# Fewer and differently issued loads at the start of a cached-attention decode kernel, and part of one multiply on GpSimd

## The chip, the cores and the metric

The kernel runs on one core of one Trainium2 chip. The metric is the device time of one execution in microseconds (us). The kernel before takes 1298.83 us (median of 3 runs, 1298.82 to 1298.9).

## The reference

One decode step for two rows of x (512 wide): attention of 32 heads over a cache of 8192 keys and values of 128 floats each, and an MLP whose SiLU gates the attention's output.

```python
def _A_ref(x, k_cache, v_cache, wq, wo):
    B, Sq, D = x.shape
    H, Dh = 32, 128
    q = (lambda x, *d: x.transpose(*d))((x @ wq).reshape(B, Sq, H, Dh), 0, 2, 1, 3)
    scores = jnp.einsum("bhqd,bhkd->bhqk", q, k_cache) * (Dh ** -0.5)
    p = _softmax(scores, axis=-1)
    o = jnp.einsum("bhqk,bhkd->bhqd", p, v_cache)
    return (lambda x, *d: x.transpose(*d))(o, 0, 2, 1, 3).reshape(B, Sq, H * Dh) @ wo

def _B_ref(x, w1, b1, w2, b2):
    y = _layernorm(x, axis=-1)
    h = _gelu(jnp.einsum("bsd,df->bsf", y, w1) + b1)
    return jnp.einsum("bsf,fd->bsd", h, w2) + b2

x = A_x
xn = _layernorm(x, axis=-1)
s = _A_ref(xn, A_k_cache, A_v_cache, A_wq, A_wo)
g = _silu(_B_ref(xn, B_w1, B_b1, B_w2, B_b2))
return x + s * g
```

Everything is float32. B is 2, D is 512, F is 1376.

## The kernel before

**Tiling.** The 64 head rows (2 batch rows of 32 heads) are worked in pairs: 32 pairs, n = 0 to 31. The keys of a pair are one tile `kb` of 128 partitions x 128 keys x 128 floats (64 KB in each partition), the values one tile `vb` of the same size. There are two `kb` buffers, which alternate (pair 0 uses the second, `kb1`), and one `vb` buffer. The first `kb` buffer holds the query weights wq until the query is made, and `vb` holds the MLP's weights w1 and w2, the biases and x, all with their scratch, until the MLP is done.

**One pair.** VectorE multiplies the keys by the query row in two halves of 64 keys (`scores_mul(n, 0)` and `(n, 1)`, L555), adds up each half over the 128 floats (`scores_sum`, L562) and takes the maximum (`max_rows`, L566). TensorE transposes the maximum (L569), VectorE makes it one number for each head (L572), ScalarE takes the exponentials (L583), and TensorE multiplies them with the values in 32 steps (`weighted`, L606).

**Order.** A planner (class `Plan`) writes each engine's operations in the order of the calls and puts in the waits that the data need. Pairs 1 to 30 run in a loop on each engine; the first and the last pair stand outside it. VectorE's order around the first pair is mul(0,0), mul(0,1), sum(0,0), sum(0,1), max(0), mul(1,0), L572 of pair 0, mul(1,1), and so on. So `weighted(0)` begins only after mul(1,0).

**Loads.** All loads are issued by SyncE (`load`, L329) into one queue, in the order w1, x, w2, b1, b2, wq, the first half and the second half of pair 0's keys (K0), then K1, V0, K2, V1, K3 and so on. K1 waits for the last TensorE operation that reads wq (L513), which stands in TensorE's order behind the whole MLP (L433 to L486). V0 waits for the last VectorE operation on the MLP's scratch and stands behind K1. K(n+2) waits for max(n), since its buffer is that of K(n); V(n) waits for `weighted(n-1)`. The last pair's keys and values come in two halves each, and the weights wo come last, in seven pieces.

**MLP and query.** x goes through two layer norms on VectorE and ScalarE (L380 to L385), TensorE transposes the results (L392), then come w1 with b1 (L433, L435), w2 with b2 (L475, L479), and the query (L513). ScalarE copies the query and spreads it to all partitions (L518, L528); mul(0,0) needs the first of these copies (`Q`, block 0) and K0's first half.

Of the kernel before, what the change touches and what calls it, by code (L numbers as in the profile page):

```python
# [5 lines left out]
ALU = mybir.AluOpType  # L6
# [155 lines left out]
                put(o, order(o.waits))  # L162


def decode_kernel(nc, x, kc, vc, wq, wo, w1, b1, w2, b2, out):
    P = 128
    B, H, S, DH = kc.shape
    D = x.shape[2]
    F = w1.shape[1]
    ND = D // P  # L170
    U = 2
    HP = P // U
    KP = S // HP
# [29 lines left out]
    def pe(fn, r=(), w=(), it=None, loop=False):  # L203
        op("pe", fn, r, w, it=it, loop=loop)
# [70 lines left out]
    def take(name, p, n, base=0, at=None):  # L275

        if at is None:
            at = used[0]
            used[0] += n
            assert used[0] <= KP * DH  # L280
        boot.append(name)
        return vb[base:base + p, at:at + n]

    w1_sb = take("w1", P, ND * F).rearrange("p (c f) -> p c f", f=F)
    w2_sb = take("w2", P, WB * P)

    at = used[0]
    take("rows", P, F + D)
    x_sb, xn, y = (take(k, B, D, 0, at + D * i) for i, k in enumerate(("x", "xn", "y")))
    b1_sb = take("b1", 1, F, R, at)  # L290
    b2_sb = take("b2", 1, D, R, at + F)
    h_row = take("h_row", B, WR * P, 2 * R, at).rearrange("b (r p) -> b r p", p=P)
    h_nat = take("h_nat", B, WB * R + WM * (QT - 1), 3 * R, at)
    hs = take("hs", P, WM * QT * QT * B).rearrange("p (a c j b) -> p a c j b", c=QT, j=QT, b=B)
# [29 lines left out]
    kf = kc.rearrange("b h s d -> (b h s d)").rearrange("(n p j d) -> n p j d", p=P, j=KP, d=DH)  # L324
    vf = vc.rearrange("b h s d -> (b h s d)").rearrange("(n p j d) -> n p j d", p=P, j=KP, d=DH)
    M = KP // 2

    def load(dst, src, sem, w, over=()):
        op("sp", lambda: nc.sync.dma_start(dst, src), (), w, over=over, dma=sem)  # L329

    def load_k(n):
        i = (n + 1) % 2
        if n in (0, N - 1):
            for s in range(2):
                load(kbuf[i][:, s * M:(s + 1) * M], kf[n][:, s * M:(s + 1) * M], f"k{i}{s}", [("kb", i, s)])
            return
        load(kbuf[i], kf[n], f"kb{i}", [("kb", i, s) for s in range(2)])
# [4 lines left out]
    CUT = D - P  # L342


    load(w1_sb, w1.rearrange("(p c) f -> p c f", p=P), "w1", ["w1"])
    load(x_sb, x.rearrange("b s d -> (b s) d"), "x", ["x"])
    load(w2_sb, w2.rearrange("f n -> (f n)").rearrange("(p e) -> p e", p=P), "w2", ["w2"])
    for t, src, k in ((b1_sb, b1, "b1"), (b2_sb, b2, "b2")):
        load(t.rearrange("o (k e) -> o k e", k=16), src.rearrange("(o k e) -> o k e", o=1, k=16), k, [k])
    load(wq_sb, wq.rearrange("(p c) n -> p c n", p=P), "wq", [("kb", 0, s) for s in range(2)])  # L350
    load_k(0)

# [73 lines left out]
    def mlp():  # L426

        chunks = range(0, F, 512)
        for f in chunks:
            w = min(512, F - f)  # L430
            ph, k = bank()
            for c in range(ND):
                pe(lambda f=f, w=w, ph=ph, c=c: matmul(ph[:B, :w], yT[:, c, :], w1_sb[:, c, f:f + w],  # L433
                                                       start=(c == 0), stop=False), ["yT", "w1"], [k])
            pe(lambda f=f, w=w, ph=ph: matmul(ph[:B, :w], ones[R:R + 1, :B], b1_sb[:, f:f + w],  # L435
                                              start=False, stop=True), ["ones", "b1"], [k])
            act(lambda f=f, w=w, ph=ph: nc.scalar.copy(h_nat[:, 1 + f:1 + f + w], ph[:B, :w]),  # L437
                [k, "h_nat"], [("h_nat", f)])

        for m in range(QT):  # L440
            dve(lambda m=m: nc.vector.tensor_copy(  # L441
                h_row[:, :, m::QT],
                h_nat[:, WM * m:WM * m + WB * R].rearrange("b (k e) -> b e k", e=WB)[:, :WR, :]),
                ["h_nat"] + [("h_nat", f) for f in chunks], [("h_row", m)])
        ph, k = bank()
        for r in range(WR):
            pe(lambda r=r: transpose(ph[:, r * B:(r + 1) * B], h_row[:, r, :], ident[2 * R:2 * R + B, 2 * R:2 * R + B]),
               ["ident"] + [("h_row", m) for m in range(QT)], [k])

        act(lambda: nc.scalar.copy(h, ph[:, :WR * B].rearrange("p (r b) -> p r b", b=B)), [k], ["h"])  # L450
        dve(lambda: nc.vector.tensor_mul(u, h, h), ["h"], ["u"])
        dve(lambda: nc.vector.tensor_scalar(u, u, GELU_A, 1.0, op0=ALU.mult, op1=ALU.add), ["u"], ["u"])
        dve(lambda: nc.vector.tensor_mul(u, u, h), ["u", "h"], ["u"])
        act(lambda: nc.scalar.activation(u, u, AF.Tanh, scale=GELU_C), ["u"], ["u"])  # L454
        dve(lambda: nc.vector.scalar_tensor_tensor(u, u, 1.0, h, op0=ALU.add, op1=ALU.mult), ["u", "h"], ["u"])
        dve(lambda: nc.vector.tensor_scalar_mul(u, u, 0.5), ["u"], ["u"])
        px, kx = bank()
        pe(lambda: matmul(px, pick, x_sb, start=True, stop=True), ["pick", "x"], [kx])
        act(lambda: nc.scalar.copy(xa, px), [kx], ["xa"])

        parts = []
        for c in range(QT):
            for lo, hi, r, m in ((0, c + 1, 1, QT - 1 - c), (c + 1, QT, 0, 0)):
                if lo == hi:
                    continue
                parts.append(("hs", c, lo))

                def part(c=c, lo=lo, hi=hi, r=r, m=m):
                    shape = [P, WM, hi - lo, B]
                    return nc.vector.tensor_tensor(  # L470
                        out=hs[:, :, c, lo:hi, :], in0=u[:, r:r + WM, :].unsqueeze(2).to_broadcast(shape),
                        in1=cls[:, m:m + hi - lo].unsqueeze(1).unsqueeze(3).to_broadcast(shape), op=ALU.mult)
                dve(part, ["u"] + [("cls", m) for m in range(QT)], [parts[-1]])
        pw, kw = bank()
        pe(lambda: matmul(pw[:R, :], b2w[R:R + 1, :], b2_sb, start=True, stop=False), ["b2w", "b2"], [kw])  # L475
        for a in range(WM):
            j = a % QT
            w = min(512, WB * P - a * 512)
            pe(lambda a=a, j=j, w=w: matmul(pw[R * j:R * (j + 1), :w], hs[:, a].rearrange("p c j b -> p (c j b)"),  # L479
                                            w2_sb[:, a * 512:a * 512 + w], start=(0 < a < QT), stop=(a + QT >= WM)),  # L480
               parts + ["w2"], [kw])
        act(lambda: nc.scalar.copy(g_sb, pw), [kw], ["g"])

        p, kp = bank()
        for c in range(QT):
            pe(lambda c=c: matmul(p[:, :P], fold[:, c, :], g_sb[:, c * P:(c + 1) * P], start=(c == 0), stop=(c == QT - 1)),  # L486
               ["fold", "g"], [kp])

        act(lambda: nc.scalar.copy(z, p[:, :P]), [kp], ["z"])
        act(lambda: nc.scalar.activation(th, z, AF.Tanh, scale=0.5), ["z"], ["th"])  # L490
        dve(lambda: nc.vector.scalar_tensor_tensor(th, th, 1.0, z, op0=ALU.add, op1=ALU.mult), ["th", "z"], ["th"])
        for j in range(QT):
            dve(lambda j=j: nc.vector.tensor_scalar_mul(
                gate[R * j:R * (j + 1), :, 1], th[R * j:R * (j + 1), j * CW:(j + 1) * CW], 0.5), ["th"], [("gate", j)])
        dve(lambda: nc.vector.tensor_tensor(
            out=xa.rearrange("p (q n) -> p q n", n=CW), in0=xa.rearrange("p (q n) -> p q n", n=CW),
            in1=slot.unsqueeze(2).to_broadcast([P, CH, CW]), op=ALU.mult), ["xa", "slot"], ["xa"])
        dve(lambda: nc.vector.tensor_reduce(out=x4, in_=xa.rearrange("p (q n) -> p n q", n=CW), axis=AX.X, op=ALU.add),
            ["xa"], ["x4"])

    mlp()


# [46 lines left out]

    def scores_mul(n, s):
        i = (n + 1) % 2
        k = kbuf[i][:, s * M:(s + 1) * M, :]
        qs = [("Q", 0)] if n == 0 else [("Q", b) for b in range(N // NB)]
        vector(n, n, lambda n: nc.vector.tensor_tensor(  # L555
            out=k, in0=k, in1=cols(Q, n * DH, DH).unsqueeze(1).to_broadcast([P, M, DH]), op=ALU.mult),
            [("kb", i, s)] + qs, [("kb", i, s)])

    def scores_sum(n, s):
        i = (n + 1) % 2  # L560
        k = kbuf[i][:, s * M:(s + 1) * M, :]
        vector(n, n, lambda n: nc.vector.tensor_reduce(out=SC[:, s * M:(s + 1) * M], in_=k, axis=AX.X, op=ALU.add),  # L562
               [("kb", i, s)], [("sc", s)])

    def max_rows(n):
        vector(n, n, lambda n: nc.vector.tensor_reduce(out=MX, in_=SC, axis=AX.X, op=ALU.max),  # L566
# [156 lines left out]
    plan.emit(HEADS)  # L723


_INS = ["A_x", "A_k_cache", "A_v_cache", "A_wq", "A_wo", "B_w1", "B_b1", "B_w2", "B_b2"]
ROWS, COLS, TOKENS, BLOCK, SLOTS = 112, 64, 2, 32, 4
_OUTS = [((ROWS, COLS), "float32")]

# [22 lines left out]
```

## Time and profile before

| What | Value |
|---|---|
| Median of 3 runs | 1298.83 us |
| Profiled execution: span from first to last instruction | 1297.6 us |
| What lies around the span (1298.83 less 1297.6) | 1.2 us |
| TensorE busy | 407.6 us (31%) |
| VectorE busy | 1138.0 us (88%) |
| ScalarE busy | 78.0 us (6%) |
| GpSimd busy | 1.4 us (0%) |
| Read from device memory over the span | 559.30 MB, 431 GB/s |

The page of the profile gives no separate time for the profiled execution besides its span; the runs' median stands 1.2 us above it. An engine's busy share says how long it works, not whether anything waits for it. The line to read first is the one on the DMA engines: their busy share in 40 equal slices of the span.

### The profile page before, as it was taken

What the parts mean: (1) busy time and instruction counts of PE and PEld (TensorE: products, weight loads), DVE (VectorE), ACT (ScalarE), POOL (GpSimd) and SP (SyncE); (2) the same over time, 40 slices, a digit from 0 to 9 for tenths busy, and PEclk for the clock granted to TensorE, in tenths of its full rate; (3) what the DMA queues carried; (4) which work ended last, traced back from release to release, by engine and by line L of the source; (5) the groups of instructions that cost most, each with busy time, mean ns of one, the idle gap of its engine ahead of it and who ended that gap; (6) DMA issues with size and microseconds to landing.
All of it is one profiled execution on the core that took longest, in us unless ns stands there. A gap on an engine that the chain in (4) does not pass through costs nothing.

```text
span 1297.6 us, 6944 instructions
## 1 busy us (share of the span) xinstructions
PE 407.6 (31%) x2796; PEld 123.4 (10%) x2796; DVE 1138.0 (88%) x294; ACT 78.0 (6%) x250; POOL 1.4 (0%) x8
## 2 busy tenths in 40 slices
PE   5703333312333312333311333321333321233328
PEld 1100110000101000101100101100001100001103
DVE  3599999988889988889988888988888988888991
ACT  1200000000000000000000000000000000000000
POOL 0000000000000000000000000000000000000000
PEclk9856666556666656666656666656666655666658
DMA  9999999999999999999999999999999999999998
GB/s 404 445 425 440 428 432 438 426 444 424 434 438 424 446 424 440 430 426 444 426 438 430 430 440 426 444 424 434 438 424 446 424 432 438 424 446 426 425 433 372
DMA packets 11231, 559.42 MB, mean 431 GB/s; under 512 B 1364, under 2 KB 1620, under 8 KB 1880
## 3 DMA queue, kind: packets, MB, share of 16 engines
q1 hardware_dynamic: 11224, 559.33, 99.7%
q8 instruction: 4, 0.07, 0.0%
q14 instruction: 3, 0.02, 0.0%
HBM read 559.30 MB, written 0.03 MB: 431 GB/s over the span
## 4 chain that ended last, share of the span: by engine, by line
DMA 71%; PE 24%; DVE 3%; issue 1%; ACT 0%; SPq 0%; DVEq 0%
DMA vb<-in_A_v_cache_dram 68%; PE po L606 22%; DMA vb<-in_A_wo_dram 2%; DVE kb L555 1%; DVE sc L562 1%; PE s L433 1%; DMA vb<-in_A_x_dram 1%; PE po L513 1%; PE s L479 0%; PE s L435 0%; DVE vb L441 0%; DVE vb L380 0%; ACT L454 0%; PE acc L696 0%; PE s L486 0%
## 5 line engine op out<-in xcount | busy, mean ns | idle before, releaser
L555 DVE TENSOR_TENSOR kb<-kb,Q 128x8192 f32<-128x8192 f32 x64 | 555.5, 8681 | 99.6 <-DMA kb<-in_A_k_cache_dram 93.1
L562 DVE TENSOR_REDUCE sc<-kb 128x64 f32<-128x8192 f32 x64 | 552.3, 8666 | 0.0
L606 PE MATMUL po<-vb,PZ 128*8 128x512 f32 x1984 | 282.3, 733 | 286.1 <-DMA vb<-in_A_v_cache_dram 284.8
L578 PE MATMUL s<-nm,srow 1*128 1x2 f32 x64 | 18.6, 358 | 360.8 <-DVE nm L572 360.8
L606 PEld LDWEIGHTS po<-vb,PZ 128*8 128x8 f32 x1984 | 56.3, 103 | 485.9 <-issue 482.4
L569 PE MATMUL s<-ident,mx 128*1 128x128 f32 x32 | 11.8, 369 | 197.8 <-DVE mx L566 197.8
L578 PEld LDWEIGHTS s<-nm,srow 1*128 1x128 f32 x64 | 15.9, 306 | 370.1 <-DVE nm L572 370.1
L613 ACT COPY o<-po 128x512 f32<-128x512 f32 x32 | 18.8, 586 | 528.2 <-PE po L606 528.2
L579 ACT COPY bias<-s 128x2 f32<-128x2 f32 x32 | 5.1, 160 | 623.9 <-PE s L578 623.9
L615 PE MATMUL s<-mod,o 128*128 128x2 f32 x256 | 33.6, 253 | 22.1 <-ACT o L613 22.1
L615 PEld LDWEIGHTS s<-mod,o 128*128 128x128 f32 x256 | 31.1, 191 | 51.4 <-ACT o L613 51.4
L583 ACT ACTIVATE PZ<-sc,bias 64x128 f32<-64x128 f32 x64 | 25.5, 399 | 1.8
L569 PEld LDWEIGHTS s<-ident,mx 128*1 128x1 f32 x32 | 2.5, 79 | 201.4 <-DVE mx L566 170.8
L621 DVE TENSOR_TENSOR Z<-blk,s 128x8 f32 (+1 forms) x32 | 5.2, 163 | 13.3 <-PE s L615 13.3
L441 DVE COPY vb<-vb 2x384 f32<-2x384 f32 x4 | 1.8, 499 | 15.4 <-ACT vb L437 15.4
L433 PE MATMUL s<-vb 128*2 128x512 f32 (+1 forms) x24 | 12.1, 654 | 0.3 <-ACT vb L393 0.3
L583 ACT ACTIVATION_READ_ACCUMULATOR PZ<-sc,bias 64x1 f32 x64 | 11.8, 185 | 0.0
L566 DVE TENSOR_REDUCE mx<-sc 128x1 f32<-128x128 f32 x32 | 9.2, 286 | 1.1
L587 ACT ACTIVATE ZR<-half,rs 128x8 f32 (+1 forms) x32 | 9.6, 301 | 4.1
L606 PE MATMUL po<-kb,PZ 128*8 128x512 f32 x64 | 9.4, 754 | 1.4 <-ACT PZ L583 1.4
L572 DVE TENSOR_REDUCE nm<-s 1x2 f32<-1x128 f32 x32 | 8.7, 272 | 0.3 <-PE s L569 0.3
L688 DVE COPY wide<-x 128x32 f32<-128x32 f32 x1 | 0.2, 195 | 9.0 <-ACT o L686 9.0
(101 smaller groups left out, 90.3 us busy)
## 6 DMA issues: line engine op xcount, KB each, us to landing
kb<-in_A_k_cache_dram SPq DMA_DIRECT2D x4, 4096.0 KB, 42.9
kb<-in_A_v_cache_dram SPq DMA_DIRECT2D x2, 4096.0 KB, 40.9
vb<-in_B_w_dram SPq DMA_DIRECT2D x2, 2752.0 KB, 12.1
vb<-in_A_wo_dram SPq DMA_DIRECT2D x1, 4096.0 KB, 19.0
vb<-in_A_wo_dram SPq DMA_DIRECT2D x1, 2048.0 KB, 23.6
vb<-in_A_wo_dram SPq DMA_DIRECT2D x1, 1280.0 KB, 26.2
vb<-in_A_wo_dram SPq DMA_DIRECT2D x2, 256.0 KB, 26.3
vb<-in_A_v_cache_dram SPq DMA_DIRECT2D x31, 29.5
```

What stands on the lines that cost most here:

```text
L433: pe(lambda f=f, w=w, ph=ph, c=c: matmul(ph[:B, :w], yT[:, c, :], w1_sb[:, c, f:f + w], start=(c == 0), stop=False), ["yT", "w1"], [k])
L513: pe(lambda i=i, c=c, wv=wv, a=a, j=j, hd=hd: matmul(PO[R * j:R * j + NQ * B, :].rearrange("m (h d) -> m h d", d=DH), xnT[:, c, a:a + NQ * ...
L555: vector(n, n, lambda n: nc.vector.tensor_tensor(out=k, in0=k, in1=cols(Q, n * DH, DH).unsqueeze(1).to_broadcast([P, M, DH]), op=ALU.mult) ...
L562: vector(n, n, lambda n: nc.vector.tensor_reduce(out=SC[:, s * M:(s + 1) * M], in_=k, axis=AX.X, op=ALU.add), [("kb", i, s)], [("sc", s)])
L566: vector(n, n, lambda n: nc.vector.tensor_reduce(out=MX, in_=SC, axis=AX.X, op=ALU.max), [("sc", 0), ("sc", 1)], ["mx"])
L569: pe(lambda i: transpose(PM[:1, :P], MX, ident), ["mx", "ident"], ["s1"], it=n, loop=n > 0)
L578: pe(lambda i: matmul(PN[:, :U], srow, NM, start=True, stop=True), ["srow", "nm"], ["s2"], **one)
L583: act(lambda i, r=r, s=s: nc.scalar.activation(PZ[r, :, s, :], sc[r], AF.Exp, bias=BIAS[r, s:s + 1], scale=SCALE, accum_out=RS[r]), ["bias ...
L587: act(lambda i: nc.scalar.activation(cols(ZR, i * UP - UP, UP), half, AF.Copy, scale=RS), ["half"] + [("rs", s) for s in range(U)], [("ZR" ...
L606: pe(lambda i, t=t, j=j, v=v: matmul(PO[R * j:R * j + U * JW, :], PZ[:, t].rearrange("p s j -> p (s j)"), v[:, t * JW:(t + 1) * JW, :].rea ...
L613: act(lambda i: nc.scalar.copy(O4, PO), ["po"], ["o4"], **one)
L615: pe(lambda i, k=k: matmul(PT[:, :U], O4[:, k * DH:(k + 1) * DH], mod[:, k:U * JW:JW], start=(k == 0), stop=(k == JW - 1)), ["o4", "mod"], ...
```

## The change

Four edits, all at the start of the kernel:

1. w1 and w2 are laid beside each other in one array in device memory, each partition's part of w1 followed by its part of w2, and come in one load (`w12`); b1 and b2 come in one load (`b12`). TensorE's first MLP product now waits for `w12`, where it waited for `w1` alone.
2. x is loaded by ScalarE's queue, ahead of ScalarE's first operation.
3. K0 comes in one load instead of two halves, so mul(0,0) waits for all of K0.
4. In the first pair, GpSimd multiplies the last 24 of the 128 keys in each partition by the query. mul(0,1) on VectorE is left with 40 keys instead of 64, and sum(0,1) waits for GpSimd too.

```diff
-    load(w1_sb, w1.rearrange("(p c) f -> p c f", p=P), "w1", ["w1"])
-    load(x_sb, x.rearrange("b s d -> (b s) d"), "x", ["x"])
-    load(w2_sb, w2.rearrange("f n -> (f n)").rearrange("(p e) -> p e", p=P), "w2", ["w2"])
-    for t, src, k in ((b1_sb, b1, "b1"), (b2_sb, b2, "b2")):
-        load(t.rearrange("o (k e) -> o k e", k=16), src.rearrange("(o k e) -> o k e", o=1, k=16), k, [k])
+    op("act", lambda: nc.scalar.dma_start(x_sb, x.rearrange("b s d -> (b s) d")), (), ["x"], dma="x")
+    load(w12_sb, w12, "w12", ["w12"])
+    load(b12_sb.rearrange("o (k e) -> o k e", k=16), b12.rearrange("(o k e) -> o k e", o=1, k=16), "b12", ["b12"])
...
-        if n in (0, N - 1):
+        if n == 0:
+            load(kbuf[i], kf[n], "k0", [("kb", i, s) for s in range(3)])
+            return
+        if n == N - 1:
...
     def scores_mul(n, s):
         i = (n + 1) % 2
-        k = kbuf[i][:, s * M:(s + 1) * M, :]
         qs = [("Q", 0)] if n == 0 else [("Q", b) for b in range(N // NB)]
+        own = M
+        if n == 0 and s == 1:
+            own = M - SHARE
+            rest = kbuf[i][:, KP - SHARE:, :]
+            pool(lambda: nc.gpsimd.tensor_tensor(
+                out=rest, in0=rest, in1=cols(Q, 0, DH).unsqueeze(1).to_broadcast([P, SHARE, DH]), op=ALU.mult),
+                [("kb", i, 2)] + qs, [("kb", i, 2)])
+        k = kbuf[i][:, s * M:s * M + own, :]
         vector(n, n, lambda n: nc.vector.tensor_tensor(
-            out=k, in0=k, in1=cols(Q, n * DH, DH).unsqueeze(1).to_broadcast([P, M, DH]), op=ALU.mult),
+            out=k, in0=k, in1=cols(Q, n * DH, DH).unsqueeze(1).to_broadcast([P, own, DH]), op=ALU.mult),
             [("kb", i, s)] + qs, [("kb", i, s)])
```

M is 64 and SHARE is 24; KP is 128. The wait of sum(0,1) for GpSimd is added in `scores_sum`.

SyncE's first loads before, each named by its tile and source (`in_B_w` is w1 or w2, `in_B_b` a bias, `in_A_k_cache` the keys); the last two rows are K1 and V0:

```order
L329 DMA vb<-in_B_w_dram 128x5504 [waits barrier_Pool_Activation_PE_DVE_SP_release]
L329 DMA vb<-in_A_x_dram 2x512
L329 DMA vb<-in_B_w_dram 128x5504
L329 DMA vb<-in_B_b_dram 1x1376
L329 DMA vb<-in_B_b_dram 1x512
L329 DMA kb<-in_A_wq_dram 128x16384
L329 DMA kb<-in_A_k_cache_dram 128x8192 x2
L329 DMA kb<-in_A_k_cache_dram 128x16384 [waits pe]
L329 DMA vb<-in_A_v_cache_dram 128x16384 [waits dve]
```

SyncE's first loads after the change:

```order
L331 DMA vb<-in_B_w_dram 128x11008 [waits barrier_Pool_Activation_PE_DVE_SP_release]
L331 DMA vb<-in_B_b_dram 1x1888
L331 DMA kb<-in_A_wq_dram 128x16384
L331 DMA kb<-in_A_k_cache_dram 128x16384
L331 DMA kb<-in_A_k_cache_dram 128x16384 [waits pe]
L331 DMA vb<-in_A_v_cache_dram 128x16384 [waits dve]
```

Eight loads ahead of K1 have become four on this queue; K1 and V0 still wait for the same engines.

VectorE's rows of the first pair before, from the last operation of the MLP to the maximum of pair 0:

```order
L498 TENSOR_REDUCE x<-vb 128x32 [waits dve]
L555 TENSOR_TENSOR kb<-kb,Q 128x8192 [waits act,dma_k10]
L555 TENSOR_TENSOR kb<-kb,Q 128x8192 [waits dma_k11]
L562 TENSOR_REDUCE sc<-kb 128x64 [waits dve] x2
L566 TENSOR_REDUCE mx<-sc 128x1 [waits dve]
```

The same place after the change:

```order
L501 TENSOR_REDUCE x<-vb 128x32 [waits dve]
L565 TENSOR_TENSOR kb<-kb,Q 128x8192 [waits act,dma_k0]
L565 TENSOR_TENSOR kb<-kb,Q 128x5120
L572 TENSOR_REDUCE sc<-kb 128x64 [waits dve]
L572 TENSOR_REDUCE sc<-kb 128x64 [waits pool,dve]
L576 TENSOR_REDUCE mx<-sc 128x1 [waits dve]
```

The first multiply waits for one load of all keys, the second has 5120 elements in each partition instead of 8192, and the second sum has a wait for GpSimd.

## Rows read from the trace of the kernel before

**Rows 1.** The page: span, busy times, DMA share in 40 slices, queue, kind: packets, MB, share.
```profile
span 1297.6 us, 6944 instructions
PE 407.6 (31%) x2796; PEld 123.4 (10%) x2796; DVE 1138.0 (88%) x294; ACT 78.0 (6%) x250; POOL 1.4 (0%) x8
...
DMA  9999999999999999999999999999999999999998
...
q1 hardware_dynamic: 11224, 559.33, 99.7%
```

**Rows 2.** Stretches: us, busy (x instructions) by engine, granted clock, DMA share, GB/s.
```profile
1.00:2.00 1.00, 0.00 (x0) 0.00 (x0) 0.63 (x10) 1.00 (x1) 0.84 (x3) 1.00 1.15 242
...
98.00:1200.00 1102.00, 321.21 (x2173) 96.84 (x2173) 1007.58 (x202) 57.77 (x199) 0.00 (x0) 0.62 1.00 433
1295.00:1297.60 2.60, 0.71 (x77) 0.58 (x66) 0.43 (x2) 0.00 (x0) 0.00 (x0) 1.00 0.05 11
```

**Rows 3.** Chain that ended last, in order of time: start us, us, what.
```profile
98.11 8.88 PE po L606 x64
...
107.01 26.88 DMA vb<-in_A_v_cache_dram
...
1226.58 29.75 DMA vb<-in_A_v_cache_dram
```

**Rows 4.** Line L329, K1 and V0 alone: duration ns, first and last start us; landings.
```profile
L329 SPq DMA_DIRECT2D kb<-in_A_k_cache_dram x1: 328/328/328, 49.8 to 49.8; - x1
L329 SPq DMA_DIRECT2D vb<-in_A_v_cache_dram x1: 431/431/431, 50.2 to 50.2; - x1
...
DMA to landing us min/median/max: 25.9/35.5/45.2
```

**Rows 5.** Line L329, K2 alone.
```profile
L329 SPq DMA_DIRECT2D kb<-in_A_k_cache_dram x1: 328/328/328, 86.8 to 86.8; - x1
...
DMA to landing us min/median/max: 27.8/27.8/27.8
```

**Rows 6.** Line L329, the eight loads issued from 0.7 to 3.6 us.
```profile
L329 SPq DMA_DIRECT2D vb<-in_B_w_dram x2: 345/366/387, 0.7 to 1.6; - x2
L329 SPq DMA_DIRECT2D kb<-in_A_k_cache_dram x2: 440/456/472, 3.0 to 3.4; - x2
...
DMA to landing us min/median/max: 9.2/33.9/52.9
```

**Rows 7.** The page's DMA issues: KB each, median us to landing.
```profile
vb<-in_B_w_dram SPq DMA_DIRECT2D x2, 2752.0 KB, 12.1
```

**Rows 8.** Line L329 from 1188.4 to 1194.5 us: the last pair's keys in halves.
```profile
L329 SPq DMA_DIRECT2D kb<-in_A_k_cache_dram x2: 328/380/432, 1188.8 to 1194.4; - x2
...
DMA to landing us min/median/max: 29.1/38.5/42.6
```

**Rows 9.** VectorE in order of time: start us, us, line [idle before <-releaser].
```profile
9.68 0.68 DVE L380 BATCH_NORM_STATS2 vb<-vb 2x6 f32<-2x512 f32 x1 [3.48 <-DMA vb<-in_A_x_dram]
...
52.27 17.29 DVE L555 TENSOR_TENSOR kb<-kb,Q 128x8192 f32<-128x8192 f32 x2 [5.90 <-ACT Q L528]
69.48 17.27 DVE L562 TENSOR_REDUCE sc<-kb 128x64 f32<-128x8192 f32 x2
86.78 0.28 DVE L566 TENSOR_REDUCE mx<-sc 128x1 f32<-128x128 f32 x1
```

**Rows 10.** TensorE in order of time.
```profile
15.05 5.94 PE L433 MATMUL s<-vb 128*2 128x512 f32 x8 [0.35 <-ACT vb L393]
...
21.87 3.59 PE L433 MATMUL s<-vb 128*2 128x512 f32 x8
```

**Rows 11.** All of GpSimd, groups by shape: busy us, mean ns.
```profile
L361 POOL MEMSET vb<- 128x512 f32 x1 | 0.5, 525 | 0.0
L362 POOL MEMSET PZ<- 128x256 f32 x1 | 0.3, 312 | 0.0
L359 POOL TENSOR_SCALAR_AFFINE_SELECT ident<-ident 128x128 f32<-128x128 f32 x1 | 0.3, 293 | 0.2 <-POOL ident L358 0.2
```

More of the change, by code (lines that the diff above doesn't have):

```diff
@@ L162, in emit, with decode_kernel @@
                 put(o, order(o.waits))
-def decode_kernel(nc, x, kc, vc, wq, wo, w1, b1, w2, b2, out):
+def decode_kernel(nc, x, kc, vc, wq, wo, w12, b12, out):
     P = 128
@@ L168, in decode_kernel @@
     D = x.shape[2]
-    F = w1.shape[1]
+    F = b12.shape[0] - D
     ND = D // P
@@ L282, in take @@
         return vb[base:base + p, at:at + n]
-    w1_sb = take("w1", P, ND * F).rearrange("p (c f) -> p c f", f=F)
-    w2_sb = take("w2", P, WB * P)
+    w12_sb = take("w12", P, ND * F + WB * P)
+    w1_sb = w12_sb[:, :ND * F].rearrange("p (c f) -> p c f", f=F)
+    w2_sb = w12_sb[:, ND * F:]
     at = used[0]
@@ L289, in decode_kernel @@
     x_sb, xn, y = (take(k, B, D, 0, at + D * i) for i, k in enumerate(("x", "xn", "y")))
-    b1_sb = take("b1", 1, F, R, at)
-    b2_sb = take("b2", 1, D, R, at + F)
+    b12_sb = take("b12", 1, F + D, R, at)
+    b1_sb, b2_sb = b12_sb[:, :F], b12_sb[:, F:]
     h_row = take("h_row", B, WR * P, 2 * R, at).rearrange("b (r p) -> b r p", p=P)
@@ L326, in decode_kernel @@
     M = KP // 2
+    SHARE = 24
     def load(dst, src, sem, w, over=()):
@@ L433, in mlp @@
                 pe(lambda f=f, w=w, ph=ph, c=c: matmul(ph[:B, :w], yT[:, c, :], w1_sb[:, c, f:f + w],
-                                                       start=(c == 0), stop=False), ["yT", "w1"], [k])
+                                                       start=(c == 0), stop=False), ["yT", "w12"], [k])
             pe(lambda f=f, w=w, ph=ph: matmul(ph[:B, :w], ones[R:R + 1, :B], b1_sb[:, f:f + w],
-                                              start=False, stop=True), ["ones", "b1"], [k])
+                                              start=False, stop=True), ["ones", "b12"], [k])
             act(lambda f=f, w=w, ph=ph: nc.scalar.copy(h_nat[:, 1 + f:1 + f + w], ph[:B, :w]),
@@ L474, in mlp @@
         pw, kw = bank()
-        pe(lambda: matmul(pw[:R, :], b2w[R:R + 1, :], b2_sb, start=True, stop=False), ["b2w", "b2"], [kw])
+        pe(lambda: matmul(pw[:R, :], b2w[R:R + 1, :], b2_sb, start=True, stop=False), ["b2w", "b12"], [kw])
         for a in range(WM):
@@ L480, in mlp @@
                                             w2_sb[:, a * 512:a * 512 + w], start=(0 < a < QT), stop=(a + QT >= WM)),
-               parts + ["w2"], [kw])
+               parts + ["w12"], [kw])
         act(lambda: nc.scalar.copy(g_sb, pw), [kw], ["g"])
@@ L562, in scores_sum @@
         vector(n, n, lambda n: nc.vector.tensor_reduce(out=SC[:, s * M:(s + 1) * M], in_=k, axis=AX.X, op=ALU.add),
-               [("kb", i, s)], [("sc", s)])
+               [("kb", i, s)] + ([("kb", i, 2)] if n == 0 and s == 1 else []), [("sc", s)])
     def max_rows(n):
@@ L723, in decode_kernel @@
     plan.emit(HEADS)
-_INS = ["A_x", "A_k_cache", "A_v_cache", "A_wq", "A_wo", "B_w1", "B_b1", "B_w2", "B_b2"]
+_INS = ["A_x", "A_k_cache", "A_v_cache", "A_wq", "A_wo", "B_w", "B_b"]
 ROWS, COLS, TOKENS, BLOCK, SLOTS = 112, 64, 2, 32, 4
@@ L737 @@
     nc = _bacc.Bacc("TRN2", target_bir_lowering=False, num_devices=1, dynamic_dma_scratch_size=4096)
+    w = [_np.asarray(inputs[k]).reshape(128, -1) for k in ("B_w1", "B_w2")]
+    laid = dict(inputs, B_w=_np.concatenate(w, axis=1),
+                B_b=_np.concatenate([_np.asarray(inputs[k]) for k in ("B_b1", "B_b2")]))
     arrays, args = {}, []
     for name in _INS:
-        a = _np.ascontiguousarray(inputs[name])
+        a = _np.ascontiguousarray(laid[name])
         arrays[f"in_{name}_dram"] = a
```

## The prediction

> **What bounds the kernel now.** The page comes first [rows 1]. VectorE is busy 88% of the span, which looks like the bound, but the row of DMA shares stands at 9 (90% or more) in 39 of 40 slices, and the one queue that carries the loads holds the 16 engines for 99.7% of the span. The stretches confirm it [rows 2]: from 1 to 2 us the first bytes flow (242 GB/s), from 98 to 1200 us 433 GB/s at a share of 1.00, and after 1295 us 11 GB/s. So the time is a start of some 2 us, a stream of 559.33 MB at 433 GB/s (1291.8 us), and a tail of some 2.6 us behind the last weights. That is 1296, close to the span of 1297.6.
>
> The chain of waits is misleading here [rows 3]. It gives a fifth of the span to L606, since each V load waits for `weighted` of the pair before. But V1, issued at 107.0, landed at 133.9, while K2, in front of it in the queue, landed only at 86.8 + 27.8 = 114.6 [rows 5]. The queue was working on K2 while V1 waited for its buffer. A wait of SyncE costs time only when the queue has run empty behind it.
>
> So for each load I need its cover: how much later it could be issued before a gap opens. The price of an empty queue is bounded by the first load, w1: issued at 0.7, landed 9.2 us later [rows 6], of which its 2752 KB (2.82 MB [rows 7]) at 433 GB/s are 6.5. So 2.7 us are start and landing. With that:
> - K1: issued 49.8, plus 2.7 is 52.5. K0's second half landed at 3.4 + 52.9 = 56.3 [rows 4, 6]. Cover 3.8 us.
> - K2: issued 86.8, plus 2.7 is 89.5; V0 landed at 50.2 + 45.2 = 95.4 [rows 4, 5]. Cover 5.9 us.
> - V1: issued 107.0, plus 2.7 is 109.7; K2 landed at 114.6 [rows 3, 5]. Cover 4.9 us.
> Later loads have more: the V load at 1226.58 took 29.75 us to land [rows 3], of which about 19.4 are its own 8.39 MB at 433 GB/s. These covers go by the last of the 16 engines; an engine that ends its share earlier could idle a little before, and no row shows by how much.
>
> **The change, part by part.**
>
> *Three loads fewer (w2, b2, half of K0).* The bytes are the same. If each load cost a start of its own, three would give back 3 x 2.7 = 8.1 us. The last pair shows what a split costs inside a full queue [rows 8]: the first half of K31 landed at 1188.8 + 38.5 = 1227.3, the second at 1194.4 + 42.6 = 1237.0, so half a tile takes 9.7 us there. The whole V load behind them landed at 1226.58 + 29.75 = 1256.3 [rows 3], 19.3 after the second half: half of that is 9.65. So a split costs 0 to 0.1 us and the three are worth 0 to 0.3. I take 0.1. The Trainium skill (SBUF — State Buffer, section "The DMA setup-cost knee") says that every transfer pays a roughly fixed 2 us whatever its size and that loads should be coalesced; by that, three loads fewer would give an estimated 6 us and a time of 1292.8. The halves land too close together for it: in this queue the fixed part lies behind the bytes of the load in front, and I follow the row.
>
> *The other side of the merge.* L433 needed w1 alone, landed at 9.9, and began at 15.05, when the layer norms were through [rows 6, 10]. Now it needs all of w12. The two weight loads have a median of 12.1 us and a minimum of 9.2 [rows 6, 7], so w2 took 15.0 and landed at 1.6 + 15.0 = 16.6. L433 is thus up to 1.5 us late, and with it the whole MLP, L513 and the issue of K1. Cover 3.8: nothing lost, 2.3 left. V0 stands behind K1 with the same delay.
>
> *x on ScalarE's queue.* x held VectorE for 3.48 us [rows 9]. Coming earlier, it can move the layer norms up by at most that, to a TensorE ready at 11.6; but w12 lands at 16.6, so nothing comes of it. If x comes no earlier, nothing is lost either. ScalarE's one issue lies ahead of a table load that nothing needs before the first layer norm. Worth 0.
>
> *K0 in one load.* mul(0,0) began at 52.27, held by the query, not by K0's first half [rows 9]. Now it waits for all of K0, 56.3: 4.0 us later. The query, up to 1.5 us late, is ready before that.
>
> *GpSimd's share.* mul(0,1) loses 24 of 64 keys: half of 17.29 us is 8.65, times 24/64 is 3.2 us off VectorE [rows 9]. GpSimd's own price is not in the trace. From below: two MEMSETs of 512 and 256 elements differ by 213 ns [rows 11], 0.83 ns an element, or 2.6 us for 24 x 128 = 3072 elements, and a memset reads nothing. From above: the AFFINE_SELECT, which reads and writes 128 elements in 293 ns, 2.29 ns an element with its fixed part, or 7.0 us. I take the upper one, since a multiply reads two inputs. Sum(0,1) needs it only after 8.65 + 5.4 + 8.6 = 22.7 us, so even 7.0 is hidden, also if GpSimd begins only when both multiplies are done (8.6 us left, one sum).
>
> *Sum for pair 0.* L566 at 86.78 moves by 4.0 - 3.2 = +0.8 us. K2 and V1 are issued 0.8 later, against covers of 5.9 and 4.9. Nothing lost. The loop then draws even, since VectorE follows the landings.
>
> So: 1297.6 + 1.2 = 1298.8, less 0.1, is **1298.7 us**. The edits trade waits on engines that the DMA stream does not wait for.
>
> **The rivals.**
>
> *Slower: GpSimd and VectorE exclude each other.* Both multiplies start on the same event and read two tensors in SBUF each. If VectorE stands still while GpSimd works, pair 0 moves by 0.8 + 7.0 = 7.8 us instead of 0.8. K2 is then late by 7.8 - 5.9 = 1.9; V1 by 7.8 - 4.9 - 1.9 = 1.0 more; together 2.9 us, 1301.6, slower by 0.22%. It decides from a standstill of 4.9 - 0.8 = 4.1 us; at the lower price of 2.6 nothing is lost. Against it: if VectorE keeps its turn, GpSimd works under the first sum, whose 8.6 us hold it. The trace has no GpSimd work beside VectorE's multiplies. The Trainium skill (SBUF — State Buffer, section "Who interferes with whom") says that a VectorE instruction with two SBUF inputs contends with a GpSimd instruction that reads SBUF, that whichever issues first blocks the other for its whole length, and that a reduce never contends; no run here shows it yet. Its page GPSIMD Engine Reference, section "Elementwise — side-by-side cycle accounting", gives 4497 ns for a 2048-element add, an estimated 6.7 us here, under my upper price.
>
> *A little slower: TensorE's clock in the MLP.* L433's first eight matmuls took 5.94 us, the next eight 3.59 [rows 10]. If the shift by 1.5 us lets such a slow spell of 2.35 fall on the MLP or L513 once more, K1 is late by 3.85, just its cover; twice, by 6.2, and 2.4 us are lost: 1301.1.
>
> *Faster: each load does pay its start.* 1298.8 - 8.1 = 1290.7. Only the first load's row speaks for it; the halves speak against.
>
> **How the numbers follow.** The forecast, no gap in the stream, gets 0.84; its own range is 1298.3 to 1299.1 (0 to 0.3 us gained, some tenths for where the 16 engines end). Exclusion gets 0.08, of which half is long enough to pass 0.2%; the clock 0.06, mostly under 2 us; the faster rival 0.02. About 0.2% (2.6 us) is what a measurement of this kernel can tell from no change. So faster 0.03, same 0.90, slower 0.07. The range leaves out the faster rival and the worst of the slow ones: 1298.2 to 1300.0.
>
> **What the profile after would show.** Right: the DMA row unchanged, one landing of w12 near 16.5, L433 shortly behind it, the first multiply at about 56, GpSimd's multiply over before the second sum, the maximum of pair 0 at 87 to 88, and landings of K1, V0, K2, V1 still some 19.4 us apart. Exclusion would show a longer multiply, or a gap before one, on VectorE in pair 0 and a landing of K2 or V1 more than 19.4 behind the one before. The clock rival would show K1 issued beyond 53.6 (49.8 plus its cover) and landing late. The prediction is wrong if the landings are evenly spaced and the time still moves by over 2.6 us.

## The result and the profile after

The changed kernel takes 1303.75 us (median of 5 runs, 1302.64 to 1304.66) against 1298.83 us (1298.72 to 1298.9): ratio 1.0038, 95% interval 1.0027 to 1.0049. It is slower by 4.9 us, where 1298.7 was forecast, and its runs lie 2.0 us apart, those of before 0.2.

The page of the changed kernel, the lines that answer to [rows 1]:

```profile
span 1301.3 us, 6943 instructions
PE 405.2 (31%) x2796; PEld 122.7 (9%) x2796; DVE 1141.1 (88%) x294; ACT 78.0 (6%) x250; POOL 16.6 (1%) x9
...
DMA  9999999999999999999999999999999999999998
...
q1 hardware_dynamic: 10930, 559.33, 99.5%
...
q10 hardware_dynamic: 4, 0.00, 0.0%
```

The profiled execution is the fastest of the five: 3.7 us above the span of before. The bytes are the same, the DMA row is the same in tenths, and the queue's share went from 99.7% to 99.5%. One slice is 32 us wide, so a hole of 3 us hides in a 9. The new queue q10 carries x.

VectorE in order of time over the first pair, for [rows 9]:

```profile
57.01 20.55 DVE L565 TENSOR_TENSOR kb<-kb,Q 128x8192 f32<-128x8192 f32 x2 [10.05 <-DMA kb<-in_A_k_cache_dram]
77.48 17.27 DVE L572 TENSOR_REDUCE sc<-kb 128x64 f32<-128x8192 f32 x2
94.78 0.29 DVE L576 TENSOR_REDUCE mx<-sc 128x1 f32<-128x128 f32 x1
```

GpSimd at the same place, and then VectorE's two multiplies apart (duration ns min/median/max, first and last start us):

```profile
57.06 15.15 POOL L561 TENSOR_TENSOR kb<-kb,Q 128x3072 f32<-128x3072 f32 x1 [54.88 <-ACT Q L531]
```

```profile
L565 DVE TENSOR_TENSOR kb<-kb,Q x2: 8693/10316/11940, 57.0 to 65.6; 128x8192 f32<-128x8192 f32 x1, 128x5120 f32<-128x5120 f32 x1
```

The two multiplies took 20.55 us, not 14.1 (8.65 + 5.4) and not even the 17.29 of before. The first, of 8192 elements, has its usual 8.69. The second, of only 5120, took 11.94. It began at 65.6; GpSimd ended at 57.06 + 15.15 = 72.2; from there to its end at 77.5 are 5.3 us, the whole of its own work. And GpSimd's 15.15 are 8.6 up to the end of the first multiply and 6.6 after it. The two engines took turns. So the maximum of pair 0 came at 94.78, 8.0 us later than before: the first multiply began 4.7 later (57.01 against 52.27), the share took 3.2 off, and the standstill of the second added 6.5.

Line L331, V0 alone and then K2 alone (for [rows 4] and [rows 5]), with the landings:

```profile
L331 SPq DMA_DIRECT2D vb<-in_A_v_cache_dram x1: 437/437/437, 50.8 to 50.8; - x1
...
DMA to landing us min/median/max: 44.9/44.9/44.9
```

```profile
L331 SPq DMA_DIRECT2D kb<-in_A_k_cache_dram x1: 327/327/327, 94.8 to 94.8; - x1
...
DMA to landing us min/median/max: 23.2/23.2/23.2
```

V0 landed at 95.7 and K2 at 118.0, 22.3 us apart; before it was 19.2 (95.4 and 114.6 [rows 4, 5]). Three microseconds of the 3.7 are here. The stretches of the changed kernel show the hole (columns as in [rows 2]), and one of them in the kernel before, below:

```profile
90.00:92.00 2.00, 0.00 (x0) 0.00 (x0) 2.00 (x1) 0.00 (x0) 0.00 (x0) 0.50 1.21 524
92.00:94.00 2.00, 0.00 (x0) 0.00 (x0) 2.00 (x1) 0.00 (x0) 0.00 (x0) 0.50 0.08 33
94.00:96.00 2.00, 0.37 (x1) 0.08 (x1) 1.74 (x3) 0.00 (x0) 0.00 (x0) 0.50 0.99 328
```

```profile
92.00:94.00 2.00, 0.00 (x0) 0.00 (x0) 2.00 (x1) 0.00 (x0) 0.00 (x0) 0.50 1.10 467
```

From 92 to 94 us the DMA share is 0.08, before it was 1.10. A packet is counted whole in the stretch in which it begins, so a share can exceed 1, and 0.08 says that hardly a packet began there; V0's last ones, begun earlier, ran until 95.3, and K2's first began at 95.7. VectorE is busy all that time, with its second sum, whose end K2 waits for: K2 was issued at 94.8, when the maximum was only beginning, so it is the sum that holds the buffer, and not the maximum.

**The theory after the result (turns, then lateness).** VectorE's multiply and GpSimd's exclude each other; that makes K2 late by 8 us, and the queue runs empty. **First rival (the loads):** the merged loads and x on a second queue cost the time. **Second rival:** GpSimd's multiply is simply slow, 15 us.

### The profile page after: what moved, and what is told of

It reads as the page before. It is cut to its first block, busy times and chain, and to the rows that moved or that the text cites. A ratio compares the mean times of both kernels' runs of the same rounds, so it can differ in the third digit from the quotient of the medians.

```text
span 1301.3 us, 6943 instructions
## 1 busy us (share of the span) xinstructions
PE 405.2 (31%) x2796; PEld 122.7 (9%) x2796; DVE 1141.1 (88%) x294; ACT 78.0 (6%) x250; POOL 16.6 (1%) x9
## 3 DMA queue, kind: packets, MB, share of 16 engines
q1 hardware_dynamic: 10930, 559.33, 99.5%
## 4 chain that ended last, share of the span: by engine, by line
DMA 67%; PE 23%; issue 5%; DVE 4%; another core or an unknown queue 0%; ACT 0%; SPq 0%; DVEq 0%
DMA vb<-in_A_v_cache_dram 63%; PE po L616 20%; DVE sc L572 3%; DMA vb<-in_A_wo_dram 2%; DVE kb L565 1%; DMA vb<-in_B_w_dram 1%; PE s L436 1%; PE po L516 1%; PE s L482 0%; PE s L438 0%; PE s L478 0%; DVE vb L444 0%; PE acc L706 0%; PE s L489 0%
## 5 line engine op out<-in xcount | busy, mean ns | idle before, releaser
L625 PE MATMUL s<-mod,o 128*128 128x2 f32 x256 | 33.6, 253 | 22.1 <-ACT o L623 22.1
L625 PEld LDWEIGHTS s<-mod,o 128*128 128x128 f32 x256 | 31.1, 191 | 51.4 <-ACT o L623 51.4
L561 POOL TENSOR_TENSOR kb<-kb,Q 128x3072 f32<-128x3072 f32 x1 | 15.1, 15147 | 54.9 <-ACT Q L531 54.9
L436 PE MATMUL s<-vb 128*2 128x512 f32 (+1 forms) x24 | 11.3, 619 | 5.7 <-DMA vb<-in_B_w_dram 5.7
## 6 DMA issues: line engine op xcount, KB each, us to landing
vb<-in_A_wo_dram SPq DMA_DIRECT2D x1, 4096.0 KB, 19.2
```

The lines of the kernel that those rows point to most:

```text
L561: pool(lambda: nc.gpsimd.tensor_tensor(out=rest, in0=rest, in1=cols(Q, 0, DH).unsqueeze(1).to_broadcast([P, SHARE, DH]), op=ALU.mult), [(" ...
L625: pe(lambda i, k=k: matmul(PT[:, :U], O4[:, k * DH:(k + 1) * DH], mod[:, k:U * JW:JW], start=(k == 0), stop=(k == JW - 1)), ["o4", "mod"], ...
```

## The experiments

All times are medians; the kernel before, beside each, had 1298.75 to 1298.78 us.

**1. The changed kernel without the share.**

```diff
-        if n == 0 and s == 1:
+        if False:
             own = M - SHARE
...
```

> The changed kernel without GpSimd's share; VectorE multiplies all 64 keys of the second half again. Theory (turns): in the changed kernel GpSimd and VectorE's second multiply excluded each other for 6.5 us, K2 was issued 8.0 us late and the load queue ran empty for 3.0 us. Without the share the maximum of pair 0 comes at 57.0 + 34.5 = 91.5 us; with 2.7 us of start that is 94.2, before V0's landing at 95.7, so K2 lands 19.4 after V0 and the time is 1299.0 to 1299.6 us. Rival (the loads): the merged loads and x on the second queue cost the time themselves; then it stays at 1302 us or more with VectorE undisturbed.

Measured: 1300.53 us (1299.31 to 1301.66), ratio 1.0014 [1.0005, 1.0023]. Between the two, outside the theory's range. VectorE was undisturbed and K2 was issued where the theory put it, but a gap was left:

```profile
90.98 0.29 DVE L576 TENSOR_REDUCE mx<-sc 128x1 f32<-128x128 f32 x1
```

```profile
L331 SPq DMA_DIRECT2D kb<-in_A_k_cache_dram x1: 327/327/327, 91.0 to 91.0; - x1
...
DMA to landing us min/median/max: 24.8/24.8/24.8
```

V0 landed at 95.2 and K2 at 115.7: 20.6 us apart, 1.2 lost, although K2 was issued 4.2 us ahead of V0's landing. The prediction wanted 2.7. The span, 1299.3 us, is 1.7 longer than before; the other 0.5 came at the kernel's end, where the first piece of wo landed 10.3 us behind the last values (9.7 before). So the share is most of the loss, and the lead that a load needs is longer than I had it.

**2. The share behind VectorE's multiplies.** GpSimd's operation is recorded after mul(0,1) and waits for it:

```diff
-                [("kb", i, 2)] + qs, [("kb", i, 2)])
+                [("kb", i, 2), ("kb", i, 1)] + qs, [("kb", i, 2)])
...
```

> The changed kernel with GpSimd's multiply made to wait for VectorE's second multiply, so that it runs under the first sum. Theory (turns): GpSimd takes 6.5 to 6.7 us alone instead of 15.1, is over before the first sum ends, the maximum comes at 57.0 + 8.65 + 5.4 + 8.6 + 8.6 = 88.3 us, no gap before K2, 1299.0 to 1299.6 us. Rival (GpSimd is slow by itself): it takes 15 us here too, the second sum waits for it until 86, the maximum comes at 95 and the time is 1302 us or more. Rival (the loads): 1302 us or more with the maximum at 88.

Measured: 1299.14 us (1298.87 to 1299.92), ratio 1.0004 [0.9995, 1.0013]. The same work on the same engines, put in another order, takes away 4.5 of the 4.9 us. VectorE in order of time, its second multiply by itself (busy us, mean ns), and GpSimd:

```profile
56.16 14.09 DVE L562 TENSOR_TENSOR kb<-kb,Q 128x8192 f32<-128x8192 f32 x2 [8.26 <-DMA kb<-in_A_k_cache_dram]
70.17 17.27 DVE L573 TENSOR_REDUCE sc<-kb 128x64 f32<-128x8192 f32 x2
87.48 0.29 DVE L577 TENSOR_REDUCE mx<-sc 128x1 f32<-128x128 f32 x1
```

```profile
L562 DVE TENSOR_TENSOR kb<-kb,Q 128x5120 f32<-128x5120 f32 x1 | 5.5, 5484 | 0.0
```

```profile
70.34 6.67 POOL L566 TENSOR_TENSOR kb<-kb,Q 128x3072 f32<-128x3072 f32 x1 [68.17 <-DVE kb L562]
```

GpSimd takes 6.67 us, not 15.1, VectorE's second multiply 5.48, not 11.94, and the sums beside GpSimd take 17.27 as always: a sum does not exclude GpSimd, a multiply does. The second rival falls.

**3. The share alone**, in the kernel before (K0 in halves, all other loads as before; GpSimd waits for the second half).

```diff
+            own = M - SHARE
...
+            pool(lambda: nc.gpsimd.tensor_tensor(
+                out=rest, in0=rest, in1=cols(Q, 0, DH).unsqueeze(1).to_broadcast([P, SHARE, DH]), op=ALU.mult),
+                [("kb", i, 2)] + qs, [("kb", i, 2)])
...
```

> The kernel before with GpSimd's share alone; weights, biases, x and the two halves of K0 as before. Theory (turns): GpSimd starts with K0's second half at 56.3, gets its turn when the first multiply ends at 60.9, holds the second until 67.5; the maximum comes at 67.5 + 5.4 + 17.3 = 90.2 us, 3.4 later than before, within K2's cover of 5.9: no gap, 1298.6 to 1299.2 us. So the share alone costs nothing; it needs the later K0 beside it. Rival (any standstill of VectorE at the start costs): 1298.8 + 3.4 = 1302.2 us.

Measured: 1299.19 us (1298.63 to 1300.98), ratio 1.0005 [0.9996, 1.0014]. Turns again, 11.45 us for GpSimd and the maximum at 90.27 as worked out:

```profile
56.24 11.45 POOL L560 TENSOR_TENSOR kb<-kb,Q 128x3072 f32<-128x3072 f32 x1 [54.07 <-DMA kb<-in_A_k_cache_dram]
```

K2, issued at 90.3, landed 19.6 us behind V0, but V1, issued at 110.6, 3.9 us ahead of K2's landing (90.3 + 24.2), landed at 110.6 + 24.6 = 135.2, 20.7 behind K2: 1.3 lost. So 3.4 us of lateness is not free, though I had expected it to be, nor does it cost 3.4; it costs 0.4 in the median, and 0 to 2.2 from run to run.

**4. Weights, biases and x alone**, in the kernel before (the load hunk of the change, with the two arrays laid side by side).

```diff
-    load(w1_sb, w1.rearrange("(p c) f -> p c f", p=P), "w1", ["w1"])
-    load(x_sb, x.rearrange("b s d -> (b s) d"), "x", ["x"])
...
+    op("act", lambda: nc.scalar.dma_start(x_sb, x.rearrange("b s d -> (b s) d")), (), ["x"], dma="x")
+    load(w12_sb, w12, "w12", ["w12"])
...
```

> The kernel before with the merged weights and biases and with x on ScalarE's queue alone; K0 in two halves, no share. Theory (turns): K1 is issued about 0.6 us later than before, within its cover of 3.8, pair 0 is worked as before, 1298.6 to 1299.4 us. Rival (the loads): 1301 us or more, and a wider spread of the runs than the 0.2 us of before.

Measured: 1299.48 us (1298.96 to 1300.25), ratio 1.0006 [0.9997, 1.0015]. That is just over the theory's range, and the runs lie 1.3 us apart, the wider spread that the rival named. Its 1301 us falls, but 0.7 us is not nothing; K1 was issued at 51.0 there instead of 49.8.

**5. x alone** on ScalarE's queue.

```diff
-    load(x_sb, x.rearrange("b s d -> (b s) d"), "x", ["x"])
+    op("act", lambda: nc.scalar.dma_start(x_sb, x.rearrange("b s d -> (b s) d")), (), ["x"], dma="x")
```

> The kernel before with x alone moved to ScalarE's queue. Weights and x together cost 0.7 us in the run before this one. If x's second queue is what costs, this one shows 1299.2 to 1299.6 us and runs more than 0.5 us apart; if the merged weights do (K1 issued 1.2 us later), this one stays at 1298.6 to 1298.9 us.

Measured: 1298.80 us (1298.62 to 1298.99), ratio 1.0 [0.9991, 1.0009]. The second queue costs nothing. It even brings VectorE forward, since x comes earlier and without the merge TensorE need not wait for all weights (L433 began at 11.49 instead of 15.05); the maximum of pair 0 comes 4.6 us earlier than before:

```profile
82.16 0.29 DVE L566 TENSOR_REDUCE mx<-sc 128x1 f32<-128x128 f32 x1
```

Nothing comes of those 4.6 us: the queue was full already.

**6. K0 in one load alone**, in the kernel before.

```diff
-        if n in (0, N - 1):
+        if n == 0:
+            load(kbuf[i], kf[n], "k0", [("kb", i, s) for s in range(2)])
+            return
+        if n == N - 1:
```

> The kernel before with K0 in one load and nothing else. The maximum of pair 0 comes at 56.3 + 34.5 = 90.8 us. Theory (a load must be issued some 4 us before the first engine ends the load in front): the engines end V0 from 92.8 on, so K2, 2 us ahead, reaches some of them late, K2 lands 19.5 to 21 us after V0, and the time is 1299.2 to 1300.8 us with runs more than 1 us apart. Rival (the cover by landings that the prediction used, 2.7 us ahead of V0's landing at 95.4 is enough): no gap, 1298.6 to 1298.9 us.

Measured: 1300.63 us (1299.3 to 1301.37), ratio 1.0012 [1.0003, 1.0021]. The cover by landings falls. Line L329, K2:

```profile
L329 SPq DMA_DIRECT2D kb<-in_A_k_cache_dram x1: 327/327/327, 90.9 to 90.9; - x1
...
DMA to landing us min/median/max: 25.9/25.9/25.9
```

V0 had landed at 48.9 + 46.2 = 95.1, K2 landed at 116.8, 21.7 later: 2.4 lost, just what this execution's span of 1300.0 has more than 1297.6. K2 was issued 4.2 us ahead of that landing.

**7. A larger share alone**: experiment 3 with 40 keys.

```diff
-    SHARE = 24
+    SHARE = 40
```

> The kernel before with a larger share alone: GpSimd multiplies 40 of the 128 keys, VectorE's second multiply is left with 24. Theory (turns): GpSimd takes 40 x 128 x 2.17 ns = 11.1 us, gets its turn at 61.1 and holds the second multiply until 72.2; the maximum comes at 72.2 + 3.3 + 17.3 = 92.8 us, when the first engines end V0, so the queue runs empty for 1 to 3 us and the time is 1300 to 1302 us, though VectorE has less to multiply than in the kernel before. Rival (no exclusion, GpSimd only slows itself down): the second multiply takes 3.3 us at once and the time is 1298.8 us.

Measured: 1301.41 us (1300.89 to 1303.67), ratio 1.0023 [1.0014, 1.0032]. VectorE is given 40 keys less to multiply than in the kernel before, and takes 5.4 us longer for it (17.29 then):

```profile
52.48 22.73 DVE L564 TENSOR_TENSOR kb<-kb,Q 128x8192 f32<-128x8192 f32 x2 [5.91 <-ACT Q L530]
```

```profile
56.31 15.68 POOL L560 TENSOR_TENSOR kb<-kb,Q 128x5120 f32<-128x5120 f32 x1 [54.13 <-DMA kb<-in_A_k_cache_dram]
```

GpSimd ended at 72.0, the 72.2 worked out from 2.17 ns an element. K2 landed 21.0 us behind V0 and V1 21.8 behind K2, together 4.0 lost, against a span 3.8 longer.

**8. The share behind the multiplies alone**: GpSimd's operation as in experiment 3, recorded after mul(0,1) and waiting for it.

```diff
-                [("kb", i, 2)] + qs, [("kb", i, 2)])
+                [("kb", i, 2), ("kb", i, 1)] + qs, [("kb", i, 2)])
...
```

> The kernel before with GpSimd's share of 24 keys alone, made to wait for VectorE's second multiply. Theory (the queue bounds the kernel): the maximum of pair 0 comes at 52.3 + 8.65 + 5.4 + 8.6 + 8.6 = 83.6 us, 3.2 earlier than before, and nothing comes of it, 1298.6 to 1298.9 us. Rival (VectorE's first pair bounds): 1295.6 us.

Measured: 1298.74 us (1298.6 to 1298.85), ratio 1.0 [0.9991, 1.0009]. The maximum came at 83.12 us, 3.7 earlier than before, for nothing. As in experiment 5, VectorE's first pair is not the bound.

**9. Weights and biases alone**: merged as in the change, x on SyncE's queue behind the weights; against experiment 4:

```diff
-    op("act", lambda: nc.scalar.dma_start(x_sb, x.rearrange("b s d -> (b s) d")), (), ["x"], dma="x")
     load(w12_sb, w12, "w12", ["w12"])
+    load(x_sb, x.rearrange("b s d -> (b s) d"), "x", ["x"])
```

> The kernel before with the merged weights and biases alone; x stays on SyncE's queue, behind the weights. x then lands with the weights near 16.6 us, the layer norms take 5.4 us from there, the first MLP product starts near 22 and K1 is issued near 55 to 56 us, when the engines have ended K0 (from 54.1 on). Theory (lateness of a load is what costs): K1 lands 21 to 23 us after K0 and the time is 1300.5 to 1302.5 us. Rival (the merge itself costs, not K1's issue): the 0.7 us of the run with weights and x, 1299.5 us.

Measured: 1303.73 us (1302.7 to 1304.37), ratio 1.0036 [1.0023, 1.005], over the range of either, and without GpSimd. The layer norms waited for x until 16.6 us, the first MLP product began at 21.99, and K1, line L331, was issued at 57.5:

```profile
L331 SPq DMA_DIRECT2D kb<-in_A_k_cache_dram x1: 327/327/327, 57.5 to 57.5; - x1
...
DMA to landing us min/median/max: 22.1/22.1/22.1
```

K0 had landed at 56.4 (2.8 + 53.6). K1 landed at 79.6, 23.3 later: 3.9 lost. K2, issued at 94.5, landed at 119.3, 20.3 behind V0 (57.9 + 41.1 = 99.0): 0.9 more. In the stretches, not a byte came from 56 to 58 us, with TensorE at work on the query:

```profile
56.00:58.00 2.00, 1.45 (x16) 0.19 (x8) 0.00 (x0) 0.49 (x1) 0.00 (x0) 1.00 0.00 0
```

This is also the cleanest price of an empty queue: 22.1 us from issue to landing, less 19.35 of transfer (the distance of two landings in a full queue, as V1 behind K2 in the kernel before), is 2.75, the 2.7 of the prediction.

**10. The changed kernel with the share behind and w1, w2 in a load each** (from the merged array).

```diff
-    load(w12_sb, w12, "w12", ["w12"])
+    load(w12_sb[:, :ND * F], w12[:, :ND * F], "w1", ["w1"])
+    load(w12_sb[:, ND * F:], w12[:, ND * F:], "w2", ["w2"])
...
```

> The changed kernel with GpSimd's multiply made to wait for VectorE's second, and with w1 and w2 in a load each again, out of the merged array; biases merged, x on ScalarE's queue, K0 in one load. Theory (lateness): K1 is issued near 45 us, nine ahead of the engines' end of K0; K2 near 87.5; no load is late and the time is the kernel's before, 1298.6 to 1298.9 us with runs within 0.4 us, against 1299.14 with the weights merged. Rival (the merged biases, x or the one load of K0 cost by themselves): 1299.1 us or more.

Measured: 1298.91 us (1298.77 to 1299.0), ratio 1.0001 [0.9992, 1.001], runs 0.23 us apart. K1 is issued at 45.0 and K2 at 87.65; the runs are as close together as before. So the one load of K0, the merged biases and x cost nothing by themselves once no load is late.

**11. The changed kernel once more.**

> The changed kernel once more, for the spread of its runs and a second profile: 1302.5 to 1304.7 us. Theory (lateness): the second multiply again ends 6.5 us late on GpSimd's account, K2 is issued at 94 to 95 us, and K2 and V1 together land 2.5 to 4 us more than 19.4 apart from the loads in front of them, differently in each execution.

Measured: 1303.40 us (1303.03 to 1304.38), ratio 1.0037 [1.0024, 1.0051]. Its profile shows the turns (GpSimd 56.5 to 71.7), K2 issued at 94.2, K2 landing 22.5 us behind V0 (117.6 and 95.1) and V1 19.8 behind K2: 3.6 lost of a span 4.1 longer. Held against the landings of the kernel before, V1 is 3.5 us late in both profiles (137.4 against 133.9). Most of the rest came long after: 0.2 in each at the first piece of wo, which landed 9.9 us behind the last values (9.7 before), and in this one 0.2 at a V load that landed at 253.9.

No version was faster than the kernel before; experiments 5 and 8 equal it within 0.03 us.

## Why the prediction was wrong

- **What bounds the kernel: right.** Where pair 0 was 3.7 and 4.6 us earlier (experiments 8 and 5) nothing was gained, and in experiments 3, 6, 7 and 9 the sum of what the landings of K1, K2 and V1 lost (1.5, 2.4, 4.0, 4.8) matches the span's growth (1.3, 2.4, 3.8, 4.9). In experiment 1 it leaves 0.5 over (1.2 of 1.7).
- **Fewer loads give 0.1 us: right in that they give nothing.** In experiments 5 and 10 loads are issued apart or together, and the time stays within 0.15 us of before. The 8.1 us of the faster rival never showed.
- **The failed step: "even 7.0 is hidden", in the part on GpSimd's share**, which let GpSimd work beside VectorE's multiplies or behind them. It did neither. It waited through the first multiply, then took its turn between the two, and VectorE stood still for 6.5 us. That was the slower rival, in its place and by its mechanism; I gave it 0.08. That its numbers come so near is partly luck. Its 7.8 us for pair 0 (measured 8.0) had the start 0.7 too early and the standstill 0.5 too long (7.0, measured 6.5). Its loss of 2.9 was 1.9 at K2 and 1.0 at V1; measured in the first profile were 3.0 at K2 and nothing at V1, 19.4 behind K2. The Trainium skill (SBUF — State Buffer, section "Who interferes with whom") said it before, and experiments 2, 3 and 7 agree with it in both halves: multiplies exclude GpSimd, sums do not (17.27 us with GpSimd beside them). I weighed it as a matter of who keeps the turn and had no row for that.
- **Why the loss is 4.9 and not 2.9: the second failed step, the covers.** I took a load to be in time when issued 2.7 us before the landing in front. That price is right for an empty queue (experiment 9), but it is not the lead that a running queue needs. The packets in the traces show a reason. The 16 engines do not end a load together: in experiment 6 they ended V0 between 92.8 and 94.7 us, the first of them 2.3 ahead of its landing at 95.1. Up to four of them then stood idle, although K2 had been issued at 90.9, and K2's first packets took up to 4.0 us, where one in the full stream takes 2.4. With 6.5 us or more of lead (K1, K2, V1 of before; K2 of experiment 2) nothing was lost. With 2.5 to 4.6 us, between 0.3 and 2.4 us were lost in experiments 1, 3, 6, 7 and 9, not in order of the lead: K2 lost 1.2 with a lead of 4.2 in experiment 1, 2.4 with the same lead in experiment 6. And V1 lost next to nothing with 3.5 in the first profile of the changed kernel, 3.4 in experiment 1 and 4.4 in experiment 9. So a short lead is where the loss can come; it does not say how large it is. With 0.9 us (K2 of the changed kernel) or none (K1 of experiment 9) it was 3.0 and 3.9. By V1's landing the first profile had lost 3.5 of its 3.7 us; the five runs lost between 3.8 and 5.8, with 4.9 the median, and that spread stays open. The prediction named the hole, "an engine that ends its share earlier could idle a little before", and put no price on it.
- **K0 in one load: "nothing lost"** fails by that step. Alone it costs 1.9 us (experiment 6). Its 4.0 us of delay would have been covered had GpSimd's share worked as counted: with the share behind the multiplies the maximum came at 87.48, against 87.6 forecast. So the costs do not add up one by one: alone the share cost 0.4 us, K0 in one load 1.9 and the weights with x 0.7, together 4.9, since they draw on the same leads.
- **The merged weights: the delay was sized rightly, its cost at 0 was too low.** L436 began at 16.83, 1.8 late against 1.5 forecast, and K1 was issued 0.3 to 1.5 us later (49.8 before; 50.1 in experiment 1, 51.4 in experiment 2), though it moves by itself too (48.5 in experiment 6, 50.0 in experiment 3, both without the merge). That costs 0.2 us beside experiment 10 and 0.7 beside experiment 5. K1 had a lead of 4.8 and 5.5 us in experiments 2 and 4; it landed in time, but V0 right behind it came at 95.8 in both (95.4 before, 95.3 in experiment 10), some 0.4 of the 0.6 us that these two executions took longer. That it is K1's lead and not the merge is argued from experiment 10, where biases and K0 stay merged, and not shown by itself.
- **x: right.** Worth 0 by itself (experiment 5). Beside the merge it is what keeps the merge from costing 4.9 us (experiments 4 and 9).
- **The clock rival did not come.** It wanted K1 issued beyond 53.6; it was issued at 50.4 and 50.7 in the two profiles of the changed kernel.

What stays open: why runs with the same late load differ by 2 us, why equal leads lose so differently, which of the 16 engines is the last one in each, and what makes the first piece of wo late.

## What to carry to other kernels

In a kernel that a load queue bounds, an engine's work matters only through the issue times of the loads that wait for it: list for each load its lead over the landing in front, and treat any edit that eats a lead away as a possible cost, even if no load is late by the price of an empty queue. Here, with loads of 8.39 MB, leads below some 6 us could lose time; elsewhere the figure has to be measured anew. Work given to a second engine is no gain before it is known that the two may run at once; where they exclude each other, order the helper under work that does not (here the sums), by a wait. A busy row in tenths of 32 us slices does not show a hole of 3 us; the distance between landings does.

## What the runs showed of the hardware

A GpSimd multiply of two tensors in SBUF and a VectorE multiply of two tensors in SBUF took turns in all four profiles in which GpSimd's did not have to wait for the end of VectorE's (after, experiments 3, 7 and 11); GpSimd, waiting, got its turn between two VectorE multiplies that stood directly behind each other, and VectorE's second one, already begun in the profile, waited. The profile counts that wait as busy time on both engines (15.15 us on GpSimd against 6.67 beside a sum, 11.94 on VectorE against 5.48 without GpSimd beside it, both in experiment 2), so a long duration there can be a wait. Beside VectorE's sums GpSimd's multiply took 2.17 ns an element (6.67 us for 3072, in experiments 2, 8 and 10 alike).
